# The first expert layer's second product, re-associated into w_out·phi for the logits and (DᵀG)·w_out for the slot inputs

## The chip, the cores and the metric

The kernel runs on one core of one Trainium2 chip. The metric is device microseconds (us) of one execution of the whole program; times shown are medians over runs, and the profile is that of one execution. TensorE (PE in the profile, PEld for its weight loads), VectorE (DVE), ScalarE (ACT) and GpSimd (POOL) each work through their own instruction list in order; SyncE (SP) issues the DMAs.

## The reference, cut to what matters

Three layers follow one another over 4608 tokens of width 512:

```python
# 1: chunked attention, batch 8, 8 heads, 9 chunks of 64 -> x [4608, 512]
# 2: first expert layer, w_in [512, 2048], w_out [2048, 512]
h = np.maximum(x @ w_in, 0.0)
x2 = h * h @ w_out
# 3: soft mixture, phi [512, 32], 8 experts with 4 slots, w1 [512, 1024], w2 [1024, 512]
logits = x2 @ phi                                  # [4608, 32]
d = np.exp(logits - logits.max(0, keepdims=True))  # over the tokens
d /= d.sum(0, keepdims=True) + 1e-09
slot_input = d.T @ x2                              # [32, 512]
for e in range(8):
    slot_out[e] = np.maximum(slot_input[e] @ w1[e], 0.0) @ w2[e]
c = np.exp(logits - logits.max(1, keepdims=True))  # over the slots
c /= c.sum(1, keepdims=True) + 1e-09
out = c @ slot_out
```

With G = h*h, x2 = G @ w_out is used in two places only, in `logits` and in `slot_input`.

## The kernel before, in words

The tokens are 36 tiles of 128. They are worked on in 13 blocks: block 0 is one tile, block 1 two tiles, blocks 2 to 12 three tiles each. The 2048 columns of `w_in` are 16 slices of 128, so a *step* is a block b with a slice f.

A step of a three-tile block does this. `moe_h` makes 12 f16 products of 384 columns (both factors are split into a high and a low f16 part, three of the four cross products are kept) into a PSUM bank `hps`, which has two buffers (L759). ACT takes the relu into `g` (L783) and squares it in place (L790). `moe_gh` and `moe_gl` split the square into `gh` (ACT, L177) and `gl` (DVE, some on POOL, L802). `moe_out` then makes nine products of 512 columns, three for each token tile, into three PSUM banks `x2_0` to `x2_2` which add up over the 16 slices (L820 to L822). `moe_out` of a step comes one step late (`LAG`): PE works on the next `moe_h` while ACT and DVE finish the square and its split. Up to block 4 the parts are fp32r, from block 5 on they are f16 and the `x` tile is scaled by its own power of two (`xmax`, `xnorm`, `xscale`).

At a block's end `moe_store` takes the three banks into `x2sb`, and `soft(b)` computes its part of the soft mixture: x2 is transposed (L1039 and L1051 in fp32, a DMA transpose and L1027 in f16) and multiplied by `phi`; the running maximum and sum over tokens (`run_m`, `run_s`) are brought up to date; the weights `dts` are transposed; dᵀx2 is made by tile products that stand beside one another in the columns of the array (L1142), and added to `acc`. The softmax over slots goes to `cmat`.

Before the main loop lies a *lead*. The weights arrive as 8-byte words and are turned into f32 and into high and low parts on the chip, one `conv(f)` for each slice: ACT L282, DVE L291, L292, L297, then a maximum, a scale, and the `wi` parts (ACT L179, DVE L330) and `wo` parts. The first nine tiles of the attention are computed there too. An order planned in advance (`list_schedule`, with the tables `RANK_T`, `RANK_F`, `RANK_S`, `SLACK` and the costs of the operations) sets the instruction lists of all engines for the lead, which covers the conversions, tiles 0 to 8 and the steps of blocks 0, 1 and 2 (`phases`, `PARTS`). The main loop works on blocks 3 to 12, 160 steps, with the attention of later tiles put between the steps; there the framework orders each engine's instructions by its own estimate of when operands are ready.

The tail: the last `soft`, `slot_inputs`, the experts' first product (L1658) and second product (L1774), the combination of the slot outputs (L1743) and the stores. w1 and w2 are 64 units of 512 KB, loaded into buffers as these fall free (`give`, `load_units`).

Of the kernel before, what the change touches and what calls it, by code (L numbers as in the profile page):

```python
# [23 lines left out]
PARTS = (9, 12)  # L24
# [5 lines left out]
RANK_T = [-144.12, -188.54, 39.7, 283.4, 80.79, 137.07, 413.6, 467.55, 52.13]  # L30
RANK_F = [94.67, 101.8, 171.24, 179.34, 179.17, -24.07, 133.94, 307.97, 133.78, 193.83, -62.63, 411.17, 364.19, -0.5, 43.44, 287.73]
RANK_S = 388.91
# [41 lines left out]
def kernel(  # L74
# [48 lines left out]
    one, least, tiny = four[:1, 0:1], four[:, 1:2], four[:, 2:4].bitcast(BF16)  # L123
# [3 lines left out]
    wo_max = const.tile([P, NF], BF16, name="wo_max")  # L127
    inv_w = const.tile([P, NF], F32, name="inv_w")
    act_w = const.tile([P, NF], F32, name="act_w")
    iv2_all = const.tile([P, NT], F32, name="iv2_all")  # L130
    cmat = None
    run_m = const.tile([3 * NS, 1], F32, name="run_m")
    run_s = const.tile([3 * NS, 1], F32, name="run_s")
    acc = const.tile([3 * NS, DM], F32, name="acc")

    wi_p, wi, wo, wo16 = {}, {}, {}, {}
    F16_FROM = 5
# [24 lines left out]
    ps_x2 = ps1.enter_context(tc.tile_pool(name="ps_x2", bufs=1, space=PSUM))  # L162
    ps_h = ps1.enter_context(tc.tile_pool(name="ps_h", bufs=2, space=PSUM))
    ps_m = ps1.enter_context(tc.tile_pool(name="ps_m", bufs=3, space=PSUM))

    def misc():
        return ps_m.tile([P, 512], F32, tag="misc", name="misc")
# [48 lines left out]
    def norm_scale(ps, am):  # L216

        pe.matmul(ps, am.to_broadcast([P, P]), am, start=True, stop=True)

    def norm_finish(ps, tag, bufs, up, down):  # L220


        gm = sm.tile([P, 1], F32, tag=tag + "g", name=tag + "g", bufs=2)
        s = sm.tile([P, 1], F32, tag=tag + "s", name=tag + "s", bufs=bufs)
        inv = sm.tile([P, 1], F32, tag=tag + "i", name=tag + "i", bufs=bufs)
        dve.tensor_scalar(gm, ps, 2.0 ** -100, 2.25, ALU.max, ALU.mult)
        dve.tensor_scalar(
            gm.bitcast(I32), gm.bitcast(I32), 24, 23, ALU.logical_shift_right, ALU.logical_shift_left
        )
        dve.tensor_scalar(  # L230
            s.bitcast(I32), gm.bitcast(I32), -1.0, float(up << 23), ALU.mult, ALU.add
        )
        dve.tensor_scalar(inv.bitcast(I32), gm.bitcast(I32), float(down << 23), None, ALU.add)
        return s, inv


    stage_sets = (("wo15", "wo14"), ("wo13", "wo12"), ("wo11", "wo10"), ("x2T", "lg"))
    stage_of = (0, 1, 2, 3, 0, 1, 2, 3, 2, 1, 3, 0, 3, 0, 3, 3)
# [5 lines left out]
    def conv(f):  # L244

# [10 lines left out]
        )  # L256
        before = [x for x in range(f) if stage_of[x] == stage_of[f]][-1:]
        holder = [
            x for x in range(f) if f"wo{f}" in stage_sets[stage_of[x]] and x not in before
# [5 lines left out]
        def value(a):  # L265
            return word(a).bitcast(F32)
# [20 lines left out]
        def join():  # L287


# [6 lines left out]
            for a in range(2):  # L296
                dve.scalar_tensor_tensor(  # L297
                    out=word(a), in0=word(a), scalar=13,
# [4 lines left out]
        for a in range(2):  # L303
            deps = [(("f", x), n) for x in before for n in ("lo", "wlo", "hi", "whi")]
# [4 lines left out]
        ops["join"] = Op("dve", 3.3, ["up0", "up1"], 2, join)  # L309

        def total():
            v["am"] = wi_max[:, f : f + 1]
            largest_of(value(0), v["am"])
# [7 lines left out]
        def hi(eng):  # L321
# [5 lines left out]
            copy(eng, wi_p[f // 2][:, f % 2, 0], value(0), v["s"])  # L327

        def lo():
            dve.scalar_tensor_tensor(  # L330
                out=wi_p[f // 2][:, f % 2, 1], in0=value(0), scalar=v["s"],
# [3 lines left out]
        def whi(eng):  # L335
            wo[f] = big.tile([P, 2, DM], F32R, tag=f"wo{f}", name=f"wo{f}")
            copy(eng, wo[f][:, 0], value(1))

        def wlo(eng):
            (dve if eng == "dve" else pool).tensor_tensor(  # L340
                out=wo[f][:, 1], in0=value(1), in1=wo[f][:, 0].bitcast(F32), op=ALU.subtract
            )
# [6 lines left out]
        deps = [(("f", x), n) for x in holder for n in ("lo", "wlo", "hi", "whi")]  # L349
        on = {"act": 0.58, "dve": 0.62, "pool": 0.7}  # L350
        ops["whi"] = Op(on, None, ["join", *deps], 4, whi)
        ops["lo"] = Op("dve", 0.68, ["hi"], 5, lo)
        ops["wlo"] = Op({"pool": 1.38, "dve": 0.61}, None, ["whi"], 5, wlo)
        for n, c in (
            ("join", 2.6), ("lo", 0.3), ("wlo", 0.4), ("hi", 0.3), ("whi", 0.3)
        ):
            ops[n].share = c
# [18 lines left out]
    def attention(i):  # L376
# [8 lines left out]
        normed = b >= F16_FROM  # L385
# [14 lines left out]
        def finish():  # L400
            v["s"], inv = pow2_finish(v["gm"], 3, "a", 5)
            v["iv"] = inv[:, 2:3]
            if not normed:
                square_of(iv2_all[:, i : i + 1], v["iv"])
# [106 lines left out]
        def xmax():  # L511
            v["xm"] = sm.tile([P, 1], BF16, tag="xm", name="xm", bufs=2)
            largest_of(v["xq"], v["xm"])

        def xnorm():
            def go(bank):
# [1319 lines left out]
```

## Time and profile before

| | |
|---|---|
| median of 3 runs | 1010.07 us (1008.98 to 1011.74) |
| span of the profiled execution | 1007.3 us |
| busy over the span | PE 94%, DVE 65%, ACT 54%, POOL 26% |
| lead, up to the last store of block 2 | 0 to 204 us |
| main loop, 160 steps | 204 to 924.7 us |
| last soft and slot inputs | 924.7 to 938.6 us |
| experts and output | 938.6 to 1007.3 us |

The profile is of one execution; its span has no row for what lies outside it, which is why the table holds both. Busy time is the union of an engine's instruction times; for PE the ends of products are modelled, so rates are read from the distance of one start to the next.

### The profile page before, as it was taken

To read this page: it belongs to the slowest core of one execution; us is meant where nothing else is said; L and a number is where in the kernel's file an instruction comes from. 1 tells how busy PE (TensorE), PEld (TensorE's weight loads), DVE (VectorE), ACT (ScalarE), POOL (GpSimd) and SP (SyncE) were. 2 spreads that over 40 slices of the span, in tenths; PEclk is the share of its full clock that TensorE was granted. 3 is DMA by queue.
4 is the path that set the end of the run, shared out by engine and by line. 5 is a ranking of instruction groups with operands and counts; after the bars stand their busy time and mean duration, and the time that the engine had idled before them with its cause. 6 is when DMAs were issued, how large, how long until landed. Compare 5 with 4: busy or idle time off the path is not lost.

```text
span 1007.3 us, 18876 instructions
## 1 busy us (share of the span) xinstructions
PE 944.1 (94%) x7277; PEld 569.9 (57%) x7277; DVE 657.1 (65%) x1395; ACT 545.9 (54%) x1038; POOL 260.1 (26%) x265
## 2 busy tenths in 40 slices
PE   6779999999999989999999999999999999999892
PEld 4667666767666655555555555555555555554352
DVE  4998965686788867676677686586776752322242
ACT  4677655455467564465555564555655644544232
POOL 3577545523223441112112111111111120000200
PEclk8799999999999999999999999999999999999896
DMA  6778232443433553344354354353343751456898
GB/s 158 222 181 194 76 126 53 74 80 73 90 65 64 118 133 64 63 72 87 63 98 83 66 119 79 63 96 64 63 95 63 149 137 50 128 176 217 271 347 253
DMA packets 270763, 117.70 MB, mean 117 GB/s; under 512 B 230224, under 2 KB 264016, under 8 KB 270672
## 3 DMA queue, kind: packets, MB, share of 16 engines
q1 hardware_dynamic: 270672, 116.49, 48.6%
q8 instruction: 57, 0.93, 0.4%
q14 instruction: 34, 0.28, 0.1%
HBM read 78.71 MB, written 9.44 MB: 88 GB/s over the span
## 4 chain that ended last, share of the span: by engine, by line
PE 70%; DVE 12%; DMA 6%; ACT 4%; issue 3%; POOL 2%; SPq 2%; DVEq 0%; POOLq 0%; ACTq 0%
PE hps L759 29%; PE x L822 10%; PE x L820 10%; PE x L821 10%; PE ehps L1658 2%; DVE qk L292 2%; DVE stage L297 2%; PE sop L1774 2%; DMA qkv<-in_q_dram 2%; DVE qk L291 1%; DMA qkv<-in_k_dram 1%; DVE gl L802 1%; PE misc L1142 1%; DMA x2T<-x 1%; DMA qkT<-qk 1%
## 5 line engine op out<-in xcount | busy, mean ns | idle before, releaser
L759 PE MATMUL hps<-xb,wi 128*128 128x384 f16 (+2 forms) x2412 | 413.3, 321 | 3.7 <-DVE wi L330 2.6
L759 PEld LDWEIGHTS <-wi 128*128 128x128 f16 x2412 | 225.5, 99 | 158.6 <-issue 16.2
L820 PE MATMUL x<-wo,gh 128*128 128x512 f16 (+1 forms) x576 | 228.3, 396 | 2.4 <-DVE x2sb L886 2.4
L821 PE MATMUL x<-wo,gh 128*128 128x512 f16 (+1 forms) x576 | 221.2, 384 | 0.0
L822 PE MATMUL x<-wo,gl 128*128 128x512 f16 (+1 forms) x576 | 206.4, 387 | 6.0 <-DVE gl L802 4.3
L802 DVE TENSOR_TENSOR gl<-g,gh 128x384 f16<-128x384 f32 (+1 forms) x162 | 96.8, 601 | 99.8 <-ACT gh L177 99.3
L783 ACT ACTIVATE g<-hps,act_w 128x384 f32<-128x384 f32 x128 | 73.9, 577 | 151.1 <-PE hps L759 137.0
L177 ACT ACTIVATE gh<-g 128x384 f16<-128x384 f32 (+3 forms) x196 | 99.6, 509 | 16.9 <-PE x L821 12.5
L479 POOL TENSOR_TENSOR ex<-ex,rs 128x512 f32<-128x512 f32 x29 | 31.4, 1081 | 293.4 <-DVE rs L476 166.7
L790 ACT ACTIVATE g<-g 128x384 f32<-128x384 f32 (+2 forms) x196 | 99.7, 509 | 5.0
L428 POOL TENSOR_SCALAR vbd<-qkv,as 64x512 f16<-64x512 f32 x58 | 53.5, 923 | 156.7 <-DVE ai L207 143.7
L171 DVE TENSOR_REDUCE am<-qkv 128x1 bf16<-128x512 f32 x94 | 63.7, 685 | 43.3 <-DMA qkv<-in_k_dram 16.2
L783 ACT ACTIVATE g<-hps,inv_w 128x384 f32<-128x384 f32 (+1 forms) x72 | 38.5, 536 | 46.6 <-PE hps L759 28.4
L822 PEld LDWEIGHTS <-gl 128*128 128x128 f16 x384 | 36.9, 98 | 45.9 <-DVE gl L802 3.9
L820 PEld LDWEIGHTS <-gh 128*128 128x128 f16 x384 | 37.5, 98 | 42.3 <-ACT g L783 5.0
L821 PEld LDWEIGHTS <-gh 128*128 128x128 f16 x384 | 37.5, 98 | 38.8 <-issue 3.5
L433 DVE SCALAR_TENSOR_TENSOR vbd<-qkv,as,vbd 64x512 f16<-64x512 f32 x58 | 54.4, 938 | 2.3 <-POOL vbd L428 1.2
L443 DVE COPY qbd<-qkT 64x1024 f16<-64x1024 f16 x58 | 25.1, 433 | 44.6 <-DMA qkT<-qk 44.2
L418 DVE SCALAR_TENSOR_TENSOR qk<-qkv,as,qk 128x512 f16<-128x512 f32 x58 | 51.0, 885 | 1.0 <-ACT qk L413 0.7
L802 POOL TENSOR_TENSOR gl<-g,gh 128x384 fp32r<-128x384 f32 (+2 forms) x39 | 42.6, 1095 | 28.8 <-ACT gh L177 20.8
L822 PEld LDWEIGHTS x<-wo,gl 128*128 128x128 f32 x192 | 35.7, 188 | 16.7 <-DVE gl L802 5.5
L469 ACT ACTIVATE ex<-ex,es 128x512 f32<-128x512 f32 x29 | 20.8, 717 | 40.3 <-DVE ex L463 40.3
(241 smaller groups left out, 1412.8 us busy)
## 6 DMA issues: line engine op xcount, KB each, us to landing
unit<-in_moe_w_dram SPq DMA_DIRECT2D x36, 512.0 KB, 4.3
unit<-in_moe_w_dram SPq DMA_DIRECT2D x56, 256.0 KB, 5.8
qkv<-in_q_dram SPq DMA_DIRECT2D x72, 128.0 KB, 3.3
qkv<-in_k_dram SPq DMA_DIRECT2D x72, 128.0 KB, 3.4
qkv<-in_v_dram SPq DMA_DIRECT2D x72, 128.0 KB, 3.3
stage<-in_moe_w_in_dram SPq DMA_DIRECT2D x16, 512.0 KB, 4.0
stage<-in_moe_w_out_dram SPq DMA_DIRECT2D x16, 512.0 KB, 5.3
out_dram<-o SPq DMA_DIRECT2D x14, 512.0 KB, 5.2
```

The lines of the kernel that those rows point to most:

```text
L171: dve.tensor_reduce(out=am, in_=src, axis=AX.X, op=ALU.max, apply_absolute_value=True)
L177: act.activation(out=out, in_=in_, func=ACTF.Copy)
L418: dve.scalar_tensor_tensor(out=qk16[:, 2 * a + 1], in0=flat[:, a], scalar=v["s"][:, a : a + 1], in1=qk16[:, 2 * a], op0=ALU.mult, op1=ALU. ...
L428: pool.tensor_scalar(out=dst[0], in0=vin, scalar1=v["s"][pr, 2:3], scalar2=1.0, op0=ALU.mult, op1=ALU.mult,)
L433: dve.scalar_tensor_tensor(out=dst[1], in0=vin, scalar=v["s"][pr, 2:3], in1=dst[0], op0=ALU.mult, op1=ALU.subtract,)
L759: pe.matmul(hp, wi[f][:, wl, kt], xb[:, xl, kt, :n], start=(nm == 0), stop=(nm == 3 * KT - 1))
L783: act.activation(out=r["g"], in_=r["hp"], func=ACTF.Relu, scale=sc)
L790: act.activation(out=g, in_=g, func=ACTF.Square)
L802: (dve if eng == "dve" else pool).tensor_tensor(out=r["gl"], in0=r["g"], in1=r["gh"] if parts16(b) else r["gh"].bitcast(F32), op=ALU.subtract,
L820: pe.matmul(o, gh[:, c], w[:, 0], start=first, stop=False)
L821: pe.matmul(o, gh[:, c], w[:, 1], start=False, stop=False)
L822: pe.matmul(o, gl[:, c], w[:, 0], start=False, stop=last)
```

## The change

x2 is no longer computed. The logits become G·(w_out·phi), with `wp` = w_out·phi made on the chip once, slice by slice, in the lead. The slot inputs become (DᵀG)·w_out: the sum over tokens is taken over G (2048 wide, kept as four quads of 512 columns) and multiplied by w_out once, in the tail.

- Dropped: `moe_gh`, `moe_gl`, `moe_out`, `moe_store`, the three `x2_*` banks, the split of w_out, the f16 form of the later blocks with its scales, the transposes of x2, its product with phi.
- Added for each slice in the lead: `w_turn` (four fp32 transposes), `w_copy`, `w_phi` (four fp32 products), `w_keep`.
- Added for each step: `moe_turn`, three fp32 transposes of g into one PSUM bank `gT` (one buffer), and `moe_keep`, an ACT copy into `G`; for each quad of four steps `moe_logits`, four fp32 products with `wp[f]`, 128*32 weights and 384 columns, one in each group of 32 columns of the array.
- `soft(b)`: `Ls`, a product with `sel4` that adds the four groups, maximum, exp, three transposes, and 12 fp32 products with G (`y`, 512 columns, four groups side by side).
- Tail: `slot_turn` (transposes) and `slot_rows_of` (16 fp32 products with w_out) ahead of `slot_inputs`. The `wo` buffers and the `G` buffers of the last block hold data until then.
- `PARTS` is (8, 8) in place of (9, 12), and the second half of block 2 moves from the lead to the main loop, which has 168 steps. The planner's tables are new. `phi` is loaded at the program's start.

```diff
-PARTS = (9, 12)
+PARTS = (8, 8)
...
-    ps_x2 = ps1.enter_context(tc.tile_pool(name="ps_x2", bufs=1, space=PSUM))
+    ps_l = ps1.enter_context(tc.tile_pool(name="ps_l", bufs=1, space=PSUM))
+    ps_t = ps1.enter_context(tc.tile_pool(name="ps_t", bufs=1, space=PSUM))
...
+    def moe_turn(b, f):
+        n = blocks[b][1]
+        g = g_of(b, f)
+        gt_ps[b, f] = ps_t.tile([P, 512], F32, tag="gT", name="gT")[:, : n * P].rearrange(
+            "p (j c) -> p j c", j=n
+        )
+        for j in range(n):
+            pe.transpose(gt_ps[b, f][:, j], g[:, j * P : (j + 1) * P], ident)
...
+    def moe_keep(b, f, eng="act"):
+        k = max(group[b], 1), f // QF
+        if k not in G_q:
+            G_q[k] = big.tile([P, 3, QF * P], F32, tag=f"G{n_G[0] % NG_RING}", name="G")
+            n_G[0] += 1
+        o0, n, c = bank0.get(b, 0), blocks[b][1], f % QF * P
+        copy(eng, G_q[k][:, o0 : o0 + n, c : c + P], gt_ps.pop((b, f)))
...
+        for x in range(QF):
+            pe.matmul(
+                L_ps[g0][NS * x : NS * x + NS, :n], wp[:, QF * q + x], g[:, x, :n],
+                start=(q == 0), stop=(q == NQ - 1), tile_position=(0, NS * x),
+                skip_group_check=True,
+            )
...
+        for j in range(n):
+            for g in range(NQ):
+                pe.matmul(
+                    y[NS * g : NS * g + NS], dd[:, j], G_q[b, g][:, j],
+                    start=(j == 0), stop=(j == n - 1), tile_position=(0, NS * g),
+                    skip_group_check=True,
+                )
...
+            slot_turn()
+            slot_rows_of()
+            give(*[(big, f"wo{x}", 1024) for x in range(NF // 2)])
             slot_inputs()
...
-    steps = [(b, f) for b in range(3, NB) for f in range(NF)]
+    steps = [(2, f) for f in range(fb, NF)] + [(b, f) for b in range(3, NB) for f in range(NF)]
...
-            moe_out(b, f, f == 0, f == NF - 1)
...
+            moe_turn(b, f)
+            moe_keep(b, f)
+            if f % QF == QF - 1:
+                moe_logits(b, f // QF)
```

PE in the main loop before, at a step of a middle block. `hps` is the bank of `moe_h`, the `x_*` are the three banks of x2, `gh` and `gl` the parts of the square.

```order
L821 MATMUL x_2_3388<-wo_645,gh 128x512
L822 MATMUL x_0_3386<-wo_645,gl 128x512 [waits DVE_49]
L822 MATMUL x_1_3387<-wo_645,gl 128x512
L822 MATMUL x_2_3388<-wo_645,gl 128x512
L820 MATMUL x_0_3386<-wo_729,gh 128x512 [waits Activation_49]
```

PE in the main loop of the changed kernel, around the end of one block's softmax. `L` is the bank of the logits (L774), `gT` that of the transposes (L757), L888 and L915 belong to `soft`, and L724 is `moe_h`, 12 products for a step.

```order
L906 MATMUL misc<-ident,dts 128x32 x3
L774 MATMUL L<-g,wp 32x384 [waits Activation_49]
L757 MATMUL gT<-ident,g 128x128 [waits Activation_49]
L757 MATMUL gT<-ident,g 128x128 x2
L774 MATMUL L<-g,wp 32x384 [waits Activation_49]
L724 LDWEIGHTS wi_948
L724 MATMUL hps<-xb_86,wi_948 128x384 [waits Activation_49]
```

and 12 products of `moe_h` later

```order
L774 MATMUL L<-g,wp 32x384 [waits Activation_49]
L888 MATMUL misc<-sel_67,Ls 128x32 [waits DVE_49]
L915 MATMUL misc<-G,dd 32x512 [waits DVE_49]
L915 MATMUL misc<-G,dd 32x512 x2
L724 LDWEIGHTS wi_948
L724 MATMUL hps<-xb_86,wi_948 128x384 [waits Activation_49]
```

Where nine products of `moe_out` stood there are now three transposes and one product of the logits; the four L774 of a quad, next to one another in the code, stand apart: the 168 of them in the main loop are in 140 runs, nearly all of a single product between products of another kind. The 12 L915 of a block stand as a run of three and a run of nine.

SP at the end of the changed kernel: the loads of w1 and w2 (`unit`). L975 and L978 are w1, L984 and L989 are w2; a row of 128x1024 or 128x4x256 is 512 KB, one of 128x512 or 128x2x256 is 256 KB.

```order
L975 DMA unit<-in_moe_w_dram 128x1024 [waits DMAHW7_49,PE_49,Activation_49]
L978 DMA unit<-in_moe_w_dram 128x512 [waits DMAHW0_49]
L989 DMA unit<-in_moe_w_dram 128x2x256 [waits DMAHW1_49]
L989 DMA unit<-in_moe_w_dram 128x2x256 [waits DMAHW2_49]
L989 DMA unit<-in_moe_w_dram 128x2x256 [waits DMAHW3_49]
L984 DMA unit<-in_moe_w_dram 128x4x256 [waits DMAHW4_49,PE_49]
```

Of the 128 half units (256 KB each), 67 stand up to the third L989 above; the last 12 of these go into the buffers of `G` that the last block's L915 frees. The eight L984 that begin with the last row go into the `wo` buffers, which `slot_rows_of` frees, and the 45 half units behind them into buffers that the experts' first product frees.

## Rows read from the trace of the kernel before

**Rows 1.** The page: busy time of each engine, and the chain by engine and line

```profile
span 1007.3 us, 18876 instructions
...
PE 944.1 (94%) x7277; PEld 569.9 (57%) x7277; DVE 657.1 (65%) x1395; ACT 545.9 (54%) x1038; POOL 260.1 (26%) x265
...
PE 70%; DVE 12%; DMA 6%; ACT 4%; issue 3%; POOL 2%; SPq 2%; DVEq 0%; POOLq 0%; ACTq 0%
```

**Rows 2.** Windows: stretch, its length, busy time by engine, granted clock, DMA share, GB/s

```profile
core 0: us, PE busy (x) PEld busy (x) DVE busy (x) ACT busy (x) POOL busy (x), PEclk, DMA share, GB/s
0.00:20.00 20.00, 10.94 (x113) 8.88 (x115) 7.57 (x20) 8.21 (x13) 6.68 (x21) 0.88 0.71 169
20.00:120.00 100.00, 84.40 (x792) 64.51 (x790) 93.34 (x150) 72.14 (x139) 63.87 (x65) 0.90 0.68 176
204.00:924.70 720.70, 707.54 (x5251) 407.59 (x5251) 476.03 (x1086) 396.71 (x759) 138.31 (x130) 1.00 0.43 92
518.20:587.30 69.10, 69.00 (x537) 38.26 (x536) 49.26 (x116) 38.40 (x72) 12.05 (x12) 1.00 0.43 81
924.70:938.60 13.90, 9.35 (x75) 5.93 (x73) 7.49 (x22) 7.93 (x18) 6.86 (x7) 0.94 0.87 291
938.60:975.40 36.80, 36.64 (x386) 16.34 (x387) 9.38 (x18) 7.41 (x14) 2.54 (x5) 0.93 0.98 315
```

**Rows 3.** Timeline of PE, one step of the last block

```profile
908.91 2.11 PE L759 MATMUL hps<-xb,wi 128*128 128x384 f16 x12
910.86 0.38 PE L820 MATMUL x<-wo,gh 128*128 128x512 f16 x1
912.80 0.49 PE L759 MATMUL hps<-xb,wi 128*128 128x384 f16 x2
```

**Rows 4.** Timeline of PE, fp32 transposes of 128x128

```profile
262.83 0.60 PE L1039 MATMUL misc<-ident,x2sb 128*128 128x128 f32 x4
263.26 0.17 PE L194 MATMUL misc<-am,ones 128*128 128x3 bf16 x1
```

**Rows 5.** Timeline of PE, fp32 products of 32 weight columns among others

```profile
385.60 0.41 PE L1051 MATMUL misc<-x2T,phi_sb 128*32 128x128 f32 x4
385.94 0.66 PE L759 MATMUL hps<-xb,wi 128*128 128x384 f16 x3
...
542.02 1.30 PE L759 MATMUL hps<-xb,wi 128*128 128x384 f16 x7
543.26 1.06 PE L1142 MATMUL misc<-x2sb,dd 128*32 128x512 f32 x6
544.25 0.39 PE L820 MATMUL x<-wo,gh 128*128 128x512 f16 x1
```

**Rows 6.** Timeline of PE, attention products of 64 columns, and their count per block

```profile
520.43 0.19 PE L454 MATMUL misc<-qkT,qbd 128*128 128x64 f16 x1
520.46 0.19 PE L455 MATMUL misc<-qkT,qbd 128*128 128x64 f16 x1
...
L507 PE MATMUL misc<-pT,vbd 128*128 128x64 f16 x24 | 2.9, 193 | 0.0
```

**Rows 7.** Groups of ACT by shape: operation, count, busy us, mean ns, idle before

```profile
L790 ACT ACTIVATE g<-g 128x384 f32<-128x384 f32 x181 | 94.3, 521 | 4.6
L783 ACT ACTIVATE g<-hps,act_w 128x384 f32<-128x384 f32 x128 | 73.9, 577 | 151.1 <-PE hps L759 137.0 <-DVE gl L802 11.3 <-PE hps L218 2.5
L1046 ACT ACTIVATE x2T<-misc 128x512 f32<-128x512 f32 x12 | 7.1, 589 | 4.7 <-PE misc L1039 4.7
```

**Rows 8.** Groups of DVE from 0 to 204 us

```profile
L297 DVE SCALAR_TENSOR_TENSOR stage<-stage,qk 128x512 int32<-128x512 int32 x32 | 27.7, 905 | 0.6
L292 DVE SCALAR_TENSOR_TENSOR qk<-qk,qk 128x1024 int32<-128x1024 f32 x16 | 23.7, 1482 | 0.6
L291 DVE TENSOR_SCALAR qk<-qk 128x1024 f32<-128x1024 f32 x16 | 16.6, 1035 | 3.4 <-ACT qk L282 3.3
L330 DVE SCALAR_TENSOR_TENSOR wi<-stage,ws,wi 128x512 f16<-128x512 f32 x16 | 14.0, 878 | 1.8 <-ACT wi L179 1.7
L171 DVE TENSOR_REDUCE wi_max<-stage 128x1 bf16<-128x512 f32 x16 | 10.8, 676 | 0.0
```

**Rows 9.** Timeline of SP (its DMAs) and PE after the main loop

```profile
933.65 37.34 SPq L1203 DMA_DIRECT2D unit<-in_moe_w_dram  x42
971.08 11.90 SPq L1758 DMA_DIRECT2D out_dram<-o  x9
...
938.60 6.20 PE L1658 MATMUL ehps<-unit,siT 128*32 128x512 f32 x32 [0.54 <-DVE siT L960]
```

More of the change, by code (lines that the diff above doesn't have):

```diff
@@ L214, in square_of @@
         )
[L216 to L238, printed above, removed]
+    stage_sets = (("wi7", "wo7"), ("wi6", "wo6"), ("wi5", "wo5"), ("G6", "lg"), ("G5", "st"))
+    stage_of = (0, 1, 2, 3, 4, 0, 1, 2, 3, 4, 1, 0, 3, 4, 3, 4)
     def slot(tag, n, dt):
@@ L256, in conv @@
         )
+        done = ("lo", "wT")
         before = [x for x in range(f) if stage_of[x] == stage_of[f]][-1:]
         holder = [
-            x for x in range(f) if f"wo{f}" in stage_sets[stage_of[x]] and x not in before
+            x for x in range(f) if f"wi{f // 2}" in stage_sets[stage_of[x]]
         ][-1:]
@@ L1062, in soft @@
         last = s0 + n == NT
-        x2 = x2sb[b]
-        nr = NS * n
-        res = {"scale": None}
-        yield from logits16(b, n, res) if F16_FROM <= b and not last else logits32(b, n, last, res)
-        lt, sc = res["lt"], res["scale"]
-        if sc is not None:
-            sc = sc[:nr]
-            if b == NB - 2:
-                give(*[(big, f"wo{NF - 1 - x}", 1024) for x in range(2)])
-        yield
-        rm = sm.tile([3 * NS, 1], F32, tag="rm", name="rm", bufs=2)[:nr]
-        nm = sm.tile([3 * NS, 1], F32, tag="nm", name="nm", bufs=2)[:nr]
@@ new lines, in soft @@
+        Ls = big.tile([P, 4, P], F32, tag="Ls", name="Ls")[:, :n]
+        dve.tensor_tensor(
+            out=Ls, in0=L[:, : n * P].rearrange("p (j t) -> p j t", j=n),
+            in1=iv.unsqueeze(2).to_broadcast([P, n, P]), op=ALU.mult,
+        )
+        bank = misc()
+        l4 = bank[:, : n * P]
+        pe.matmul(
+            l4, sel4.rearrange("p a s -> p (a s)"), Ls.rearrange("p j t -> p (j t)"),
+            start=True, stop=True,
+        )
+        yield
+        rm = sm.tile([P, 1], F32, tag="rm", name="rm", bufs=2)
@@ L1099, in soft @@
+        if not last:
+            dve.tensor_copy(run_m, rm)
+        dve.scalar_tensor_tensor(
+            out=run_s, in0=run_s, scalar=al, in1=rsum, op0=ALU.mult, op1=ALU.add
+        )
+        if last:
+            c_two(0)
         nonlocal cmat
@@ L1327, in step_ops @@
             "sq": Op(cost_of("square", P * n), None, ["relu"], 0, lambda e: moe_square(b, f, e)),
[L1328 to L1335 removed]
+            "T": Op("pe", 0.11 * n + 0.1, ["sq"], 0, lambda: moe_turn(b, f)),
+            "ev": Op(cost_of("read", P * n), None, ["T", *held], 0, lambda e: moe_keep(b, f, e)),
+        }
+        if f % QF == QF - 1 and b:
+            also = [(("s", 0, f), "sq")] if b == 1 else []
+            deps = ["sq", *also, *[(("f", f - x), "wpc") for x in range(QF)]]
+            ops["lg"] = Op("pe", 0.8, deps, 0, lambda: moe_logits(b, f // QF))
         return ops
@@ L1428, in list_schedule @@
             best = None
-            for e in free:
+            for strict, e in [(x, e) for x in (True, False) for e in free]:
+                if best is not None and not strict:
+                    break
                 cands = []
@@ L1607 @@
                         )
[L1608 to L1609 removed]
+                    give((big, "g0", 1536))
                 gen = soft(b)
@@ L1617 @@
     ps2 = ctx.enter_context(tc.tile_pool(name="ps2", bufs=1, space=PSUM))
-    late = ctx.enter_context(tc.tile_pool(name="late", bufs=1))
-    siT, sel4, second = (fin[x] for x in ("siT", "sel4", "second"))
+    siT, second = fin["siT"], fin["second"]
     hT_g, hps_g = {}, {}
```

589 lines of the change are left out of this document (180 added, 409 removed).

## The prediction

> **What bounds the kernel now.** I read first the page's busy times and its chain [rows 1]: PE is busy 944.1 of 1007.3 us, and 70% of the chain is PE work. An average over stages says little, so the windows come next [rows 2]. In the main loop (204 to 924.7 us, 160 steps) PE is busy 707.5 of 720.7 us, while DVE has 476 and ACT 397; a middle block (518.2 to 587.3) has PE at 69.0 of 69.1 us at a granted clock of 1.00. So there the sum of PE's work is the time. In the lead it is otherwise: between 20 and 120 us PE has 84 of 100 us and DVE 93, and DVE's list is what the conversions and the first attention tiles are waiting for. After the main loop the DMA share is 0.87 and then 0.98 [rows 2], and SP issues loads of w2 from 933.65 until the first store of the output at 971.08 [rows 9]: the tail goes at the pace of the loads.
>
> So I price the change three times: PE in the main loop, DVE in the lead, loads in the tail.
>
> **PE in the main loop, removed.** A step of the last block begins at 908.91, its nine x2 products at 910.86, the next step at 912.80 [rows 3]: 1.95 us for twelve h products (0.1625 each) and 1.94 us for nine x2 products. The latter all go.
>
> **PE in the main loop, added or kept.** The changed loop has 168 steps of three tiles.
> - h: 2016 products at 0.1625 give 327.6 us.
> - Transposes of g: four fp32 transposes take 262.83 to 263.26 [rows 4], 0.109 each with the next row's start as their end; 504 of them give 54.9 us.
> - The logits' products are not in the trace of before in this size. The nearest rows are fp32 products of 32 weight columns [rows 5]. Three of them side by side, 512 columns, leave PE from 543.26 to 544.25, 0.99 us; the same with 128 columns from 385.60 to 385.94, 0.34 us. Between these, 384 columns take 0.77. Before the first one PE loses more: seven h products from 542.02 would end at 543.16, the product begins at 543.26. That is 0.10, in all 0.87 us for a group, whether one product or several columns of the array are in it. The four products of a quad could share one group, but in PE's list the 168 stand in 140 runs, because each was put where its square is ready. 140 × 0.87 = 121.8 us. The bounds: 42 groups of four would be 36.5 us; 168 single ones 146 us.
> - Attention of 27 tiles: 48 products of 64 columns a tile (24 rows for each of six lines in a block of three tiles), 0.029 apart [rows 6], 37.6 us; with the small reductions 41.
> - Softmax of 11 blocks: the product with sel4 0.7, transposes of dts 0.35, the 12 products with G as a run of three (0.99 + 0.10) and one of nine, three deep (3 × 0.87 + 0.2), slot logits about 0.7; 5.7 a block, 62.7 us.
>
> The sum is 608 us. Before, idle was 13.2 of 720.7 us, 1.8% [rows 2]. Now more rows of PE wait for ACT: each logits product stands right where its square should be ready, and the transposes need the one gT bank back. I take about twice the share, 4%, 24 us: **main loop 632 us** (720.7 before, for eight steps fewer). Bounds for the waits: nothing, and 10% or 60 us.
>
> Is another engine next? A block takes PE some 58 us. ACT had 38.4 us in the middle block [rows 2]; it loses the copy gh and gains the copy of the transposes out of PSUM, which lies between 0.52 and 0.59 (square and x2T copy [rows 7]), and loses the work on x2: not more than 39. DVE had 49.3 and loses gl. Both are hidden under PE, if nothing in their order is late.
>
> **Page against rows.** The Trainium skill, TensorEngine Tiling (Array Packing), Theoretical Speedup, gives up to 4× for a dimension of 32 or less; by it the logits would be 36.5 us and the total some 85 us lower. The same page, Key Properties, says that changing the tiling mode drains TensorE. The 0.10 ahead of L1142, and the part of the 0.34 that doesn't shrink with columns, agree with the second rule; the first needs neighbours that PE's list doesn't have.
>
> **The lead.** It loses eight of its 32 step-equivalents, gl, the x2 stores and the split of w_out. What stays on DVE is the conversions: 27.7 + 23.7 + 16.6 + 14.0 + 10.8 = 92.8 us [rows 8] and some 10 of small ones, and the nine tiles with about 38: 141 us in all. The first 20 us have 7.6 of them as now [rows 2]; the other 133 at the present share, 93 of 100 us, end at 163. PE can begin with the main steps while DVE is on the last tile, so I set **the lead at 160 us** instead of 204 (150 to 185). The new transposes, copies and products with phi, 16 times some 3 us over PE and ACT, lie under DVE.
>
> **The tail.** Before, it was 82.6 us from 924.7. The change holds back the buffers: in SP's list 55 of 128 half units go before the last block's G is free, 12 more with it, eight whole units behind slot_rows, and 45 half units behind the experts' product. So 73 halves, 19.1 MB, are loaded after the last y. That y comes some 9 us after the last step (sel4, maximum, exp, transposes, 12 products). Before, 42 halves, 11.0 MB, were issued in 37.4 us [rows 9], a rate of 0.294 MB/us, and the window shows 315 GB/s [rows 2]; at 0.3 to 0.35 the 19.1 MB take 55 to 64 us. The last load is then issued 64 to 73 us after the main loop; now it is 971.1 − 924.7 = 46.4 us. I take +18.5: **tail 101 us**. What is won in PE's sum is partly paid back here.
>
> **The sum.** 160 + 632 + 101 = 893 us of span. The profiled execution has 1007.3 against a median of 1010.07, 2.8 more: 896 us.
>
> **Rivals.**
> - *The logits' products are cheap after all* (they overlap with their neighbours, or drift into packs on the chip): 36.5 instead of 121.8, 811 us. Against it: the list is in order, and [rows 5] show the loss also for groups between h products.
> - *Waits take the place.* The attention chain runs through DMA, DVE, ACT and POOL in order; if blocks cannot go faster than 66 us instead of 60.6 (58.3 with 4%), the main loop is 688 us and the total 952; at the old 69.1, 984. For it: in rows of before the gaps are small because PE was slower than all the others. Against it: ACT and DVE at 39 of 58 us.
> - *A lower clock.* The main loop is at 1.00 now, the stretch 20 to 120 us at 0.90 [rows 2]. At 0.90 the 608 us become 676, total 963. The Trainium skill, TensorE: Matmul & The Clock Gate, Part 4, says that transposes do not count as a busy PE in the same way; no run here shows that yet, and transposes are 9% of PE's sum.
> - *Slower: the single gT bank makes each step a round trip.* If PE had to wait for h, relu, square, transposes and copy in turn, a step would cost 1.95 + 0.58 + 0.52 + 0.33 + 0.55 and some handing over, about 4.4 us; 168 of these and the other 226 us of PE make a main loop of 965 and a total of 1229. It decides against the change from 0.68 us of exposed wait a step on (114 us over 168). Against it: the transposes stand one step behind, so relu and square (1.10) fit under the next h (1.95).
> - *No change*: it would need two of the losses at once.
>
> **How the numbers follow.** Forecast (PE's sum with waits up to 10%): 0.70. Cheap logits products: 0.07. Waits or clock, still faster: 0.15. Within 0.3% of before, which is about what a measurement of this kernel can tell from no change: 0.02. Slower: 0.06. Faster is thus 0.92. For the range I add the bounds: the logits without the loss around them (−31), waits as before (−13), lead −10 or +20, waits at 10% (+37), clock or attention (+56). All of them at one end are unlikely, two or three are not: 840 to 972 us.
>
> **What would show it.** In the profile after: h products 1.95 us a step; L774 alone with 0.87 from its start less the loss ahead to the next row; a main loop of 632 us with PE above 95%; the first step of block 2's second half near 150 us; loads without a gap from the last y on to the output, some 67 us. The prediction is wrong if PE shows waits for ACT of more than 0.4 us a step, if L774 costs under 0.5, or if the lead ends by DMA or PE instead of DVE.

## The result and the profile after

The changed kernel takes 895.46 us in the median (895.40 to 895.71 over 4 runs) against 1009.53 before: a ratio of 0.8866 with the 95% interval 0.8854 to 0.8879. The forecast was 896 us. The profiled execution has a span of 893.3 us.

The page after, busy times and chain, beside [rows 1]:

```profile
span 893.3 us, 16464 instructions
...
PE 821.1 (92%) x6556; PEld 468.7 (52%) x6556; DVE 442.6 (50%) x927; ACT 466.4 (52%) x949; POOL 179.8 (20%) x210
...
PE 72%; DVE 8%; DMA 8%; ACT 5%; issue 3%; SPq 2%; POOL 1%; DVEq 0%; POOLq 0%; ACTq 0%
PE hps L724 37%; PE L L774 11%; PE gT L757 7%; PE misc L915 4%; DMA unit<-in_moe_w_dram 3%; PE ehps L1427 1%; DMA qkv<-in_k_dram 1%; ACT G L185 1%; DVE qk L273 1%; SPq L363 1%; DMA qkT<-qk 1%; PE misc L856 1%; PE misc L443 1%; DMA pT<-p 1%; PE misc L888 1%
```

The chain is still PE. In place of the nine x2 products, half of each old step [rows 3], the logits (L774), the transposes (L757) and the products with G (L915) hold 22% of the span.

The windows after (stretch, length, busy time by engine, granted clock, DMA share, GB/s), cut at the first step that the main loop has now and at the last logits product; they answer to [rows 2]:

```profile
20.00:154.20 134.20, 119.16 (x1195) 92.15 (x1195) 110.83 (x207) 96.35 (x199) 30.93 (x38) 0.91 0.66 171
...
154.20:789.80 635.60, 617.88 (x4659) 331.61 (x4656) 298.79 (x653) 335.20 (x688) 133.81 (x143) 0.99 0.40 87
789.80:893.30 103.50, 72.56 (x612) 35.49 (x609) 24.97 (x48) 26.48 (x51) 9.28 (x11) 0.86 0.90 296
```

| us | before | forecast | after |
|---|---|---|---|
| lead | 204 | 160 | 154.2 |
| main loop | 720.7 (160 steps) | 632 | 635.6 (168 steps) |
| tail | 82.6 | 101 | 103.5 |

PE is busy 617.9 of 635.6 us in the main loop: read by its busy time, its sum is still the time there (experiments 1, 3 and 11 test it). The tail gave back 21 us of what the other two won.

The timeline of PE inside a middle block, where the cost of a logits product can be read off (start, busy us, engine, line, operation, shape and count, idle before; one logits product shows as two passes, x2); [rows 3] showed a step of before, [rows 5] the products from which the price was taken:

```profile
446.37 2.12 PE L724 MATMUL hps<-xb,wi 128*128 128x384 f16 x12
448.42 0.83 PE L774 MATMUL L<-g,wp 128*32 128x384 f32 x2
449.18 0.41 PE L888 MATMUL misc<-sel,Ls 128*128 128x32 f32 x2
449.52 1.06 PE L915 MATMUL misc<-G,dd 128*32 128x512 f32 x6
450.51 1.31 PE L724 MATMUL hps<-xb,wi 128*128 128x384 f16 x7
451.75 0.83 PE L774 MATMUL L<-g,wp 128*32 128x384 f32 x2
452.52 0.34 PE L724 MATMUL hps<-xb,wi 128*128 128x384 f16 x1
452.69 0.49 PE L757 MATMUL gT<-ident,g 128*128 128x128 f32 x3
453.02 0.81 PE L724 MATMUL hps<-xb,wi 128*128 128x384 f16 x4
```

Twelve products from 446.37 end at 448.32 by their distance of 0.1625; the logits product starts at 448.42 and the next row at 449.18. That is 0.10 + 0.76 = 0.86 us for one product of 32 weight columns. Three transposes cost 0.33 (452.69 to 453.02). They are fp32 too, and begin only 0.01 us behind the h product of 452.52 (0.1625 long): this speaks against the step from f16 to fp32 as the cause of the 0.10.

### The profile page after: what moved, and what is told of

The parts are those of the page before. It is cut to its first block, busy times and chain, and to the rows that moved or that the text cites. A ratio compares the mean times of both kernels' runs of the same rounds, so it can differ in the third digit from the quotient of the medians.

```text
span 893.3 us, 16464 instructions
## 1 busy us (share of the span) xinstructions
PE 821.1 (92%) x6556; PEld 468.7 (52%) x6556; DVE 442.6 (50%) x927; ACT 466.4 (52%) x949; POOL 179.8 (20%) x210
## 4 chain that ended last, share of the span: by engine, by line
PE 72%; DVE 8%; DMA 8%; ACT 5%; issue 3%; SPq 2%; POOL 1%; DVEq 0%; POOLq 0%; ACTq 0%
PE hps L724 37%; PE L L774 11%; PE gT L757 7%; PE misc L915 4%; DMA unit<-in_moe_w_dram 3%; PE ehps L1427 1%; DMA qkv<-in_k_dram 1%; ACT G L185 1%; DVE qk L273 1%; SPq L363 1%; DMA qkT<-qk 1%; PE misc L856 1%; PE misc L443 1%; DMA pT<-p 1%; PE misc L888 1%
## 5 line engine op out<-in xcount | busy, mean ns | idle before, releaser
L724 PE MATMUL hps<-xb,wi 128*128 128x384 f16 (+2 forms) x2400 | 417.7, 322 | 0.9 <-ACT g L739 0.4
L724 PEld LDWEIGHTS <-wi 128*128 128x128 f16 x2400 | 223.2, 99 | 186.9 <-issue 66.4
L185 ACT ACTIVATE G<-gT 128x384 f32<-128x384 f32 (+1 forms) x200 | 95.1, 475 | 176.4 <-PE gT L757 170.1
L739 ACT ACTIVATE g<-hps,inv_w 128x384 f32<-128x384 f32 (+1 forms) x200 | 109.9, 567 | 75.5 <-PE hps L724 70.3
L774 PE MATMUL L<-g,wp 128*32 128x384 f32 x384 | 122.7, 498 | 0.0
L757 PE MATMUL gT<-ident,g 128*128 128x128 f32 x576 | 102.8, 286 | 15.9 <-ACT G L185 14.8
L757 PEld LDWEIGHTS gT<-ident,g 128*128 128x128 f32 x576 | 67.5, 144 | 50.9 <-ACT G L185 22.8
L468 POOL TENSOR_TENSOR ex<-ex,rs 128x512 f32<-128x512 f32 x28 | 29.9, 1068 | 170.7 <-DVE rs L465 149.6
L507 DVE SCALAR_TENSOR_TENSOR xb<-misc,xb 128x512 f16<-128x512 f32 x29 | 19.8, 683 | 55.3 <-ACT xb L501 55.2
L915 PE MATMUL misc<-G,dd 128*32 128x512 f32 x288 | 46.3, 632 | 0.6 <-ACT G L185 0.6
L481 POOL TENSOR_TENSOR p<-ex,p 128x512 f16<-128x512 f32 x29 | 35.6, 1229 | 36.7 <-ACT p L478 36.0
L402 ACT ACTIVATE qk<-qkv,as 128x512 f16<-128x512 f32 x58 | 38.6, 719 | 5.3 <-DVE as L212 5.3
L774 PEld LDWEIGHTS L<-g,wp 128*32 128x32 f32 x384 | 20.7, 108 | 38.6 <-issue 31.1
```

What stands on the lines that cost most here:

```text
L185: act.activation(out=out, in_=in_, func=ACTF.Copy)
L402: act.activation(out=qk16[:, 2 * a], in_=flat[:, a], func=ACTF.Copy, scale=v["s"][:, a : a + 1])
L724: pe.matmul(hp, wi[f][:, wl, kt], xb[:, xl, kt], start=(nm == 0), stop=(nm == 3 * KT - 1))
L739: act.activation(out=g, in_=hp, func=ACTF.Relu, scale=sc)
L757: pe.transpose(gt_ps[b, f][:, j], g[:, j * P : (j + 1) * P], ident)
L774: pe.matmul(L_ps[g0][NS * x : NS * x + NS, :n], wp[:, QF * q + x], g[:, x, :n], start=(q == 0), stop=(q == NQ - 1), tile_position=(0, NS * x),
```

## The experiments

All times are medians; the changed kernel is 895.46. The kernel before, run again beside the experiments, took 1010.2 to 1011.9 us, so a difference of some 2 us between runs says little. For each run "lead", "main loop" and "tail" are cut as above, each at its own first step, in its profiled execution. Where "start to next" is said, the distance from each of a kind's starts to the next start on PE is summed over the main loop, idle time included.

**1. The four logits products of a quad side by side.**

```diff
-                moe_logits(b, f // QF)
+                with tc.issue_after(last_T[0].ins):
+                    moe_logits(b, f // QF)
```

> The changed kernel with one thing added: the four logits products of a quad are queued on PE behind the transposes of the quad's last step, so that they stand next to one another. Nothing is left out. In the trace of the changed kernel a lone logits product costs 0.093 us ahead of it, 0.346 for its two passes and 0.418 up to the next product, 0.857 in all, and the main loop has some 136 runs of them. Theory (PE's sum is the time of the main loop, and a group of four costs what one costs): 136 runs become some 43, 93 x 0.857 = 80 us less, 815 us; the main loop falls to about 545 us. Rival (another engine or the attention chain takes over as soon as PE is shorter): less than 30 us are won, 865 us or more, and PE shows the difference as idle time. Rival (the loss around a group is per product and not per group): no change, 895 us.

Measured: 836.6 us (832.15 to 838.9), 59 less. The logits products' start-to-next sum falls from 107.9 us (141 runs) to 48.2 (43 runs), 12 us of idle time included; where no idle time follows, the group of four takes 0.785 us to the next start (the median), and one product took 0.765:

```profile
402.69 0.49 PE L758 MATMUL gT<-ident,g 128*128 128x128 f32 x3
403.11 0.85 PE L775 MATMUL L<-g,wp 128*32 128x384 f32 x8
```

Eight passes (four products) take 0.85 us of busy time, where the two passes of one product took 0.83. So the loss is per group, and the third theory is out. But PE's idle time in the main loop rises from 17.7 to 48.7 us, and the waits of PE say for what (line, what it waited for, us in total, times, longest):

```profile
PE misc L443 <- DVE qbd L432: 13.7, 9, 2.5
PE misc L495 <- DMA pT<-p: 10.5, 9, 2.0
PE hps L725 <- ACT xb L501: 7.8, 6, 1.7
```

PE now reaches attention products before their inputs are there. The main loop fell by 50.3 us while its idle time rose by 31.0, so PE's work fell by 81: 79 for the logits with what stands ahead of them, the 80 of the first theory, and 8 more since the products with G stand in fewer runs here too (38.0 to 29.9 us start to next), less 6 that transposes, attention and softmax gained. Of these 81 the rival took 31. Another 7 us came off the tail.

**2. A second bank for the transposes.** In blocks 3 to 12 odd steps use the bank of the second logits tile.

```diff
-            L_ps[g0] = ps_l.tile([P, 512], F32, tag=f"L{g0 % 2}", name="L")
+            L_ps[g0] = ps_l.tile([P, 512], F32, tag=f"L{g0 % 2 if g0 < 3 else 0}", name="L")
...
+        second = 3 <= b < NB and f % 2
+        gt_ps[b, f] = (ps_l if second else ps_t).tile(
+            [P, 512], F32, tag="L1" if second else "gT", name="gT"
```

> The changed kernel with a second PSUM bank for the transposes of g in blocks 3 to 12: the second logits bank is not needed there, so odd steps use it. Nothing is left out. In the changed kernel PE sits idle 12.8 us of the main loop ahead of the transposes for ACT's copy out of the bank, and some 3 us at the end of the last block. Theory (PE's sum plus small waits): those waits go, 10 to 17 us less, 879 to 885 us. Rival (the single bank is a round trip that each step pays, also where the trace calls it something else): over 40 us less, below 855. Rival (the wait moves to the next dependence on ACT): less than 5 us, 890 us or more.

Measured: 852.83 us (851.55 to 854.13), 43 less: by the figure alone that is the round trip. The trace says otherwise: PE's idle before transposes falls from 12.8 to 2.4 us, as the first theory has it, and a large part of the rest is in another place. The 12 products with G of a block now stand in one run in 11 of 11 blocks, not in 21 runs, and their start-to-next sum falls from 38.0 to 29.9. That asked for a run of its own, experiment 3.

**3. Only the products with G in one run.**

```diff
+        with tc.issue_after(last_T[0].ins) if not last else ExitStack():
             for j in range(n):
                 for g in range(NQ):
```

> The changed kernel with one thing added: the 12 products of a block's softmax with G are queued on PE behind the transposes that are listed last when they are written, so that they stand as one run of 12 instead of a run of three and one of nine. Nothing is left out. It is one part of what the second transpose bank brought along. Theory (each run pays for itself): the start-to-next time of these products falls from 38.0 to about 30 us, as in the runs with two banks, and the total by 6 to 10 us, to 885 to 889. Rival (the run waits for the later transposes, and gives back what it wins): 892 us or more.

Measured: 874.16 us (870.74 to 876.37), 21 less where 6 to 10 were expected, all in the main loop (616.1). The products themselves fell to 29.9 us as expected, 8.1 less; the rest is around them: logits 5.2 (134 runs for 141), transposes 4.0, others 2. If the two effects add, experiment 2 is this run's 21 us and another 21 us of its own: 14.8 in the main loop (10 of it in the transposes) and 5.8 in the tail. That is a little above the 10 to 17 that the single bank was priced at, and half of the 40 that a round trip paid by each step would have shown.

**4. Both.** Experiments 1 and 2 together.

> Both edits together. Theory of PE's sum: the gains add, 90 to 97 us less, 798 to 806 us. Rival (with PE shorter, ACT's order is what blocks wait for): the second bank brings clearly more here than alone, or packing clearly less, so that the sum of the two gains is missed by over 15 us.

Measured: 812.33 us (810.58 to 816.67), 83 less. The two gains, 59 and 43, would be 102; 19 are missing, which is the rival's mark of over 15; but 8 of them are missing because both runs contain the same gain on the products with G, and 11 remain. In the main loop (76.6 us shorter) PE's idle time is 32.5 us, where the changed kernel has 17.7; 16.5 of it stands ahead of attention products, which wait for DMA transposes and VectorE. What took the place is thus mostly the attention chain, not the order of ACT that the rival named. The theory's number (90 to 97) was missed by 7.

**5. The attention set out earlier**, experiment 4 with `first_use[b] - 14` turned into `- 18`, and then into `- 24`.

> Packed logits and two transpose banks, and the attention operations of a tile set out four steps earlier in the main loop. Nothing is left out. With both edits the trace had PE idle 16.5 us of the main loop ahead of attention products, for DMA transposes of p and for VectorE's copies. Theory (these products are listed too close behind what they wait for): 10 to 16 us less than 812, 796 to 802. Rival (the two buffers of a tile hold the chain, so that an earlier place brings no earlier data): within 4 us of 812.

Measured: 807.32 us (805.2 to 809.22): 5 less, not 10 to 16, and just outside the rival's 4. PE still waits for the transposes of p:

```profile
PE misc L495 <- DMA pT<-p: 12.9, 14, 1.6
```

> Packed logits and two transpose banks, and the attention of a tile set out ten steps earlier than in the changed kernel (four steps earlier was 807 us, not earlier 812). Nothing is left out. With four steps PE still waited 12.9 us for DMA transposes of p. Theory (listed too close behind what they wait for): that wait falls below 5 us and the total to 795 to 803. Rival (the two buffers of a tile, or the scheduler's own estimate of the DMA's time, set the distance): PE still waits over 10 us for them, 804 to 812 us.

Measured: 859.19 us (857.92 to 862.68), 47 more than experiment 4; neither theory has it. By the kernel's list the result of a block's first tile is then written to the x buffer, one of two, some 22 steps ahead of that block's first step, so ahead of the last steps of the block that still uses this buffer: these steps are computed with the next tiles' x, and above all they wait for it:

```profile
PE hps L725 <- ACT xb L501: 22.9, 17, 3.2
PE misc L443 <- DVE qbd L432: 11.9, 4, 7.7
PE misc L495 <- DMA pT<-p: 10.3, 2, 7.8
```

The wait for p stays over 10 us. What sets the distance between p's transposes and their users stays open.

**6. No step of lag.** `LAG = 0`, and each step's h products queued behind the last step's transposes.

```diff
-    LAG = 1
+    LAG = 0
...
-            moe_h(b, f)
+            with tc.issue_after(last_T[0].ins) if last_T[0] else ExitStack():
+                moe_h(b, f)
```

> The changed kernel, but in the main loop the transposes of a step stand ahead of the next step's products in PE's order, so that relu and square (0.57 and 0.52 us) and the handing over between engines no longer have the next 1.95 us of products over them. Nothing is left out. If nothing else covered this, some 1.4 us x 168 = 235 us would be added, 1130 us; the logits, attention and softmax products (some 200 us in all) can stand in the gap. The rival of the prediction that ends slower than before needs 0.68 us of exposed wait a step. Expected: 940 to 1100 us, and the wait of PE's transposes for ACT rises from 13 us to over 60. If it stays below 910, the step-late order isn't what kept that rival away.

Measured: 1019.99 us (1019.46 to 1020.92), a ratio to the kernel before of 1.0087 (1.0069 to 1.0105): about as long as before, if anything a little longer. The timeline of PE:

```profile
500.84 0.55 PE L758 MATMUL gT<-ident,g 128*128 128x128 f32 x3 [0.82 <-ACT g L747]
501.23 2.11 PE L725 MATMUL hps<-xb,wi 128*128 128x384 f16 x12
503.27 0.83 PE L775 MATMUL L<-g,wp 128*32 128x384 f32 x2
```

and the largest wait of PE:

```profile
PE gT L758 <- ACT g L747: 99.3, 125, 3.2
```

Between the h products and their transposes the square is late, 99 us in all. 131 us in the main loop, 0.78 us a step, take away the whole gain of the change; the rival that ends slower was priced to decide from 0.68 us a step on. Of the 131, idle time is 103 (0.61 a step); the other 28 are PE's own work, most of it logits products that stand in 177 runs here (141 in the changed kernel).

**7. Slack on the other engines.** Four multiplications on GpSimd per step, on a scratch tile that nothing reads.

```diff
+            for _ in range(4):
+                pool.tensor_tensor(out=spare, in0=spare, in1=spare, op=ALU.mult)
```

> The changed kernel with four extra multiplications of 160 columns on GpSimd in each step of the main loop, on a scratch tile that nothing reads. Nothing is left out. It asks two things. First, is there slack in the attention chain under PE: by PE's sum the time stays within 5 us of 895; rival, the chain through DVE and GpSimd is what blocks wait for: over 15 us more. Second, why DVE's operations on two SBUF inputs were shorter after the change (the long one of the conversion 1.24 us against 1.48, the low part of qk 0.80 against 0.89): if it is because GpSimd was idle beside them, the low part of qk and the second half of vbd in the main loop go back up to 0.88 us or more here, with nothing else changed for them; if not, they stay at 0.80.

Measured: 925.51 us (922.37 to 928.52), 30 more, which reads like the rival. By stages it isn't: the main loop is 635.2 us, as in the changed kernel; the lead is 185.1 instead of 154.2. Nothing holds these operations back: of 672, 203 stand in the lead, in front of squares and conversions that GpSimd has there, as this piece of its timeline shows:

```profile
138.18 18.79 POOL L1362 TENSOR_TENSOR spare<-spare 128x160 f32<-128x160 f32 x25
157.07 1.12 POOL L220 TENSOR_SCALAR iv_all<-ai 128x1 f32<-128x1 f32 x1
158.26 6.06 POOL L1362 TENSOR_TENSOR spare<-spare 128x160 f32<-128x160 f32 x9
164.29 0.83 POOL L748 TENSOR_TENSOR g<-g 128x384 f32<-128x384 f32 x1
```

The main loop thus has slack on GpSimd for the 226 us of extra work that stand from 205 to 780 us. For the second question the groups of DVE from 205 to 780 us, first of the changed kernel:

```profile
L422 DVE SCALAR_TENSOR_TENSOR vbd<-qkv,as,vbd 64x512 f16<-64x512 f32 x51 | 40.4, 793 | 6.3 <-POOL vbd L417 5.6
L407 DVE SCALAR_TENSOR_TENSOR qk<-qkv,as,qk 128x512 f16<-128x512 f32 x50 | 38.2, 786 | 2.7 <-ACT qk L402 2.3
```

and of this run:

```profile
L1362 POOL TENSOR_TENSOR spare<-spare 128x160 f32<-128x160 f32 x444 | 225.9, 509 | 31.6
...
L422 DVE SCALAR_TENSOR_TENSOR vbd<-qkv,as,vbd 64x512 f16<-64x512 f32 x54 | 45.3, 839 | 3.2 <-POOL vbd L417 2.3
L407 DVE SCALAR_TENSOR_TENSOR qk<-qkv,as,qk 128x512 f16<-128x512 f32 x54 | 44.2, 835 | 2.7 <-ACT qk L402 2.2
```

0.79 to 0.84 us: up, but not to the 0.88 that was set as the mark. A part of it is shown, no more.

**8. The work on w_out·phi in the lead.** Made for one slice only.

```diff
+        if f:
+            for n, c in (("join", 2.6), ("lo", 0.3), ("hi", 0.3)):
+                ops[n].share = c
+            return ops
         ops["wT"] = Op("pe", 0.6, ["join", *late_], 5, w_turn)
```

> The changed kernel with w_out times phi made for the first slice only and used for all 16, which leaves out 15 of 16 of the four transposes, four products and two copies that the lead gained; the order of the lead is planned anew for it. Prediction's claim (this work lies under DVE and the loads): the first step of block 2's second half starts within 4 us of 154 us and the total is within 5 us of 895. Rival (PE and ACT in the lead have no room for it): 16 times up to 3 us come off, the lead ends 15 to 45 us earlier.

Measured: 904.02 us (899.82 to 904.52), 8.6 more; the lead is 166.2 instead of 154.2 with less work in it. The planner made another order, and the rows from 20 to 120 us show less on PE and a lower granted clock than in the changed kernel (85.26 us, 0.89):

```profile
20.00:120.00 100.00, 57.60 (x679) 44.96 (x676) 89.08 (x163) 62.78 (x123) 19.35 (x23) 0.76 0.75 198
```

The rival's 15 to 45 us are not there, but order and work were changed together, so this run does not price the work. The next one keeps the order.

**9. VectorE shorter in the lead, the same lists.**

```diff
-            largest_of(value(), v["am"])
+            largest_of(value()[:, :16], v["am"])
```

> The changed kernel, with the maximum that sets the scale of a w_in slice taken over 16 of its 512 columns, which leaves out the rest of that reduction; every engine's instruction list is the same as in the changed kernel, only 16 operations of VectorE in the lead are shorter, 0.68 us each down to about 0.1. It asks what bounds the lead. The prediction's step (VectorE's list, at a 93% share): 16 x 0.58 = 9 us off, the first step of block 2's second half at 145 instead of 154 us, total near 886. Rival (VectorE at 83% and PE at 89% of the stretch from 20 us on: PE and the loads set the pace as much): 0 to 4 us off, 891 us or more.

Measured: 895.36 us (889.37 to 895.86), no change, and the lead 154.3. The 16 operations took 2.5 us (10.8 in the changed kernel), and the window from 20 us on shows VectorE 8.4 us lower and nothing won:

```profile
20.00:154.20 134.20, 119.63 (x1189) 92.28 (x1185) 102.41 (x205) 95.70 (x198) 30.06 (x38) 0.89 0.65 171
```

So the sum of VectorE's work does not bound the lead after the change.

**10. The tail's loads.** Seven wo buffers given to units early, slot_rows on the first two slices for all.

```diff
-                    ps[NS * g : NS * g + NS], yT[:, c, g], wo[QF * g + c],
+                    ps[NS * g : NS * g + NS], yT[:, c, g], wo[(QF * g + c) % 2],
...
-    at(40, lambda: give((big, "st", 1024)))
+    at(40, lambda: give((big, "st", 1024), *[(big, f"wo{x}", 1024) for x in range(1, NF // 2)]))
```

> The changed kernel, but the product with w_out in the tail uses only the first two slices of w_out for all 16, which leaves out most of that product's data and none of its work, so that seven of the eight wo buffers can take units of w1 and w2 from the early main loop on. 3.67 MB of loads move from the tail into the main loop. Theory (the tail from the last y on goes at the pace of the loads, 0.35 MB per us): 3.67 / 0.35 = 10.5 us less, 885 us, nearly all of it after the main loop. Rival (the tail is set by the chain of PE, ACT and DVE through the slot inputs, the two expert products and the output): less than 3 us.

Measured: 887.4 us (886.18 to 890.13), 8.1 less; in the profiled executions the main loop is 1.0 longer and the tail 9.9 shorter, against 10.5 expected. SP's timeline, first of the changed kernel:

```profile
805.34 1.75 SPq L975 DMA_DIRECT2D unit<-in_moe_w_dram  x4
...
811.79 10.10 SPq L984 DMA_DIRECT2D unit<-in_moe_w_dram  x8
821.99 35.68 SPq L989 DMA_DIRECT2D unit<-in_moe_w_dram  x45
858.05 9.30 SPq L1527 DMA_DIRECT2D out_dram<-o  x9
```

and of this run:

```profile
848.42 10.16 SPq L1527 DMA_DIRECT2D out_dram<-o  x9
```

The output begins 9.6 us earlier. The tail goes at the pace of the loads.

**11. The kernel before, with two thirds of x2's products.**

```diff
-            pe.matmul(o, gh[:, c], w[:, 1], start=False, stop=False)
```

> The kernel before, with the products of gh with the low part of w_out left out, three of the nine x2 products of each step; this drops a small part of the result's precision and nothing else. It asks whether PE's sum was the time in the old main loop as the prediction read it. Theory: 32 steps at 3 x 0.234 and 128 steps at 3 x 0.2155 us are 105 us less in the main loop, which falls from 720.7 to about 616 us, and the total to 905; the lead hardly moves. Rival (behind PE stood waits for the split of the square on ACT and VectorE that come out as PE gets shorter): less than 70 us, 940 us or more.

Measured: 921.45 us (920.02 to 925.37), 90 less than the kernel before beside it (1011.92), where 105 were expected from PE's sum and under 70 from the rival; the window that was 720.7 us ends some 86 us earlier:

```profile
204.00:840.00 636.00, 607.49 (x4768) 352.68 (x4767) 474.24 (x1087) 398.28 (x763) 150.61 (x130) 0.99 0.49 104
```

PE's idle time there is 28.5 us, 13.2 before [rows 2]. Of the 105 us taken from PE's sum some 15 came back as waits. PE's sum was the time of the old loop in the main, but with little to spare behind it.

## Why the prediction was right, point by point

**The main loop by PE's sum: right, though not in each term.** Start to next, in us, forecast and measured: h 327.6 and 341.1, logits 121.8 and 107.9, transposes 54.9 and 81.3, attention 41 and 48.0, softmax 62.7 and 57.2, waits 24 and (within the others) 17.7. The sum was 632, measured 635.6. The logits' price was right, 0.87 forecast and 0.86 read; some 0.1 of it stands ahead of the product and is counted with its neighbour here, mostly with h, whose own products keep their 0.1625. (The row of 128 columns in [rows 5] has four passes, two products and not three; the 0.77 read between the rows held all the same.) The transposes were under-sized by 26 us: the 0.109 of [rows 4] holds inside a run of three, but 12.8 us of idle time for the one gT bank come on top, and three of them ahead of a logits product or a product with G take 0.47 us to the next start instead of 0.33 (37 runs, 5 us); the rest was not broken down. The waits, twice the old share, were set a little high. (In the rival of waits the figures of a block stand the wrong way round: 60.6 us is the one with the 4%, 58.3 the one without.) The errors cancel, which is luck: no single term is as good as their sum.

**The cost that stands around a product of few columns: shown.** Experiment 1 takes away 98 of 141 runs and 60 us of the logits' sum. The Trainium skill, TensorEngine Tiling (Array Packing), Key Properties, says that changing the tiling mode drains TensorE; the 0.10 us ahead of L774 and the unchanged cost of a group of four agree.

**The rival that ends slower: kept away by the step of lag, shown** by experiment 6: without the lag a step is 0.78 us longer, 0.61 of it idle time, and the gain is gone. Experiments 2 and 3 show that the one bank costs some 20 us as it is, not a round trip per step.

**The lower clock: not there.** The main loop has 0.99 with the transposes in it.

**The lead: the number right by luck, the reason wrong.** The step that failed is "DVE's list is what the conversions and the first attention tiles are waiting for": the forecast 160 us came from 141 us of VectorE's work at a share of 93%. Both were too high and cancel. VectorE's work up to 154.2 us was 119 us (the conversion's five groups took 92.8 us [rows 8], and 77.9 after: 21.4 + 11.9 + 11.9 + 11.0 + 10.9 + 10.8), and its share from 20 us on is 83%, below PE's 89%. The 93% was that of 20 to 120 us alone; the rest of the old lead stood on PE already then, as this window of the kernel before shows (PE first, VectorE third):

```profile
120.00:204.00 84.00, 81.74 (x558) 57.51 (x558) 52.43 (x85) 43.61 (x78) 41.79 (x39) 1.00 0.31 76
```

Experiment 9 settles it for VectorE: 8 us less work there, and the lead stays. Near the end of the lead PE has next to no idle time in the changed kernel, against VectorE's 15.9:

```profile
120.00:140.00 20.00, 19.91 (x136) 13.35 (x136) 15.92 (x28) 14.80 (x31) 1.34 (x3) 0.93 0.36 118
```

Of the signs that the prediction named for being wrong, this one came up: the lead ends by PE instead of DVE. What bounds the first 100 us, the planned order, loads or the granted clock, is not settled, and whether the new work on w_out·phi lies hidden is not shown; experiment 8 changed too much at once.

**The tail: right.** 101 forecast, 103.5 measured, for the reason given: experiment 10 moves 3.67 MB and wins 9.9 us there, 0.37 MB/us. Inside it two terms were off and cancel: the loads go on 15.5 us after the main loop (805.34 less 789.8) where 9 were forecast, and the 73 half units from there to the output take 52.7 us where 55 to 64 were. The +18.5 that was taken lies near the low end of what the prediction's own figures give, 17.6 to 26.6; the output began 68.2 us after the main loop, 46.4 before, which is 22 more.

**The better version.** Packed logits, two transpose banks and the attention four steps earlier (experiment 5) take 807.3 us, 0.798 of the kernel before (0.7958 to 0.8006). The rival of cheap logits products named 811 us. Packing them by their order did bring what PE's sum says, but 31 us of it went into waits, and packing alone stops at 836.6; that 811 is reached with the second bank's help is a coincidence of numbers.

## What to carry to other kernels

When one engine's sum is the time, price a change by the distance from start to start on that engine, switches of shape included, and look in its list where the new instructions stand: four small products apart cost four times what four together cost. Each us taken off such an engine brings others' waits nearer, 31 of 81 us in experiment 1, 15 of 105 in experiment 11. A stage's reason is not proved by its length: shorten the engine that is named, with all lists kept, before building on it.

## What the runs showed of the hardware that had not been expected

VectorE's operations in the conversion got shorter though their shapes did not change. The groups of DVE from 0 to 160 us after the change:

```profile
L273 DVE SCALAR_TENSOR_TENSOR qk<-qk,qk 128x1024 int32<-128x1024 f32 x16 | 21.4, 1339 | 0.5
L278 DVE SCALAR_TENSOR_TENSOR stage<-stage,qk 128x512 int32<-128x512 int32 x16 | 11.9, 741 | 0.6
L272 DVE TENSOR_SCALAR qk<-qk 128x1024 f32<-128x1024 f32 x16 | 11.0, 686 | 5.0 <-ACT qk L262 5.0
```

They were 1482, 905 and 1035 ns [rows 8]. Beside them GpSimd was busy 63.9 us from 20 to 120 us before [rows 2], and 25.7 after. In the lead of experiment 7 GpSimd is busy 86.5 of these 100 us, and the same groups from 0 to 160 us read:

```profile
L273 DVE SCALAR_TENSOR_TENSOR qk<-qk,qk 128x1024 int32<-128x1024 f32 x16 | 21.8, 1361 | 0.5
...
L272 DVE TENSOR_SCALAR qk<-qk 128x1024 f32<-128x1024 f32 x16 | 13.1, 819 | 6.4 <-ACT qk L262 6.3
L278 DVE SCALAR_TENSOR_TENSOR stage<-stage,qk 128x512 int32<-128x512 int32 x16 | 13.0, 814 | 0.6
```

L278 goes about half the way back (its other 16, into `wo`, go from 683 to 936) and L272 more than a third, while the long L273 hardly moves. In the main loop of experiment 7 two other operations rose by 6%. So work on GpSimd beside it makes VectorE's operations longer, but it is not all of the difference: in experiment 8, with GpSimd at 19.35 us, L272 took 784 ns. The Trainium skill, GPSIMD Engine Reference, Specifications, says that GpSimd shares its SBUF interfaces with VectorE and contends with instructions on two SBUF inputs or in a two-port mode. The direction agrees for L278 and for the two operations of the main loop; L273, on two inputs too, does not show it, and why it got shorter stays open.
